# Sorting one batch item's values from both halves of the partitions, in a fused Sinkhorn attention and maxout kernel

## The chip, the cores and the metric

The kernel runs on one core of a Trainium2 chip. The metric is the device time of one execution in microseconds (us), lower is better; a result is the median of several executions, and beside it stands one execution taken with the hardware profiler. All input loads from HBM and the store of the output are within that time.

## What is computed

There are 4 batch items of 8 heads, 768 tokens and 64 dimensions a head. The tokens are cut into 8 blocks of 96. Five rounds of Sinkhorn turn each head's 8 x 8 `sort_net` into a mixing matrix P; keys and values are mixed block by block with P ("sorted"); each query block attends to the sorted block with its own number; the result, with the heads side by side, goes through a maxout layer.

```python
for _ in range(5):
    P = np.exp(P - np.max(P, axis=-1, keepdims=True))
    P = P / (np.sum(P, axis=-1, keepdims=True) + 1e-09)
    P = P / (np.sum(P, axis=-2, keepdims=True) + 1e-09)
k_sorted = np.einsum('bhij,bhjcd->bhicd', P, k_b)
v_sorted = np.einsum('bhij,bhjcd->bhicd', P, v_b)
attn = softmax(scale * q_b @ k_sorted^T)      # per block of 96
x = (attn @ v_sorted), heads side by side     # 3072 tokens x 512
out = np.maximum(x @ w1, x @ w2) @ w_out      # 512 -> 1024 -> 512
```

## The kernel before

**The algebra.** `max(h1, h2) = max(h1 - h2, 0) + h2`. So the kernel keeps W1 - W2 in place of W1 (`w_difference`), computes h = x (W1 - W2) with a ReLU as the eviction (`moe_h`, lines 591 to 617), and adds x (W2 Wout) to the output product. W2 Wout is made once: W2 is transposed on TensorE (`w2_transposes`, L553), then four products of 8 matmuls each (`w_product`, L571 to L584) fill PSUM two to a tile; each second product is followed by one eviction of 1024 columns into `wc`. An output tile of 128 tokens is 12 matmuls, 8 with g and 4 with x, in two parts of 6 (`moe_out`, L625).

**The sort on TensorE.** For a batch item the 64 rows (head, block) of v stand on 64 partitions: item b uses rows 0 to 63 if it is even and 64 to 127 if odd. `load_v` (L154) fills `v_raw`, and `turn_v` (L209) copies it to `v_dc` with d ahead of the token within the block. A sort is then, for each d, one matmul whose weights are 64 rows of `v_dc` (96 tokens, loaded 128 wide by `v_weights`) and whose moving operand is a 64 x 64 block diagonal matrix of P. `sort_v` (L411) does this for items 0 and 1, 16 values of d to a PSUM tile, all from one row half. `sort_v_pair` (L431) does it for items 2 and 3 together: 8 values of d from each row half, the halves in turn. `sort_k` (L387) sorts the keys from both halves in turn.

**The block diagonals.** `block_diagonals(b)` (L293) multiplies a selection matrix (`sel_v`, `sel_k`, made by `selections`, L281) with P on TensorE (L303), masks the result on VectorE with `maskJ` (L313), sums it (L320), and multiplies with `maskM` (L323) into bf16 matrices `bd`. For item 0 it runs ahead of everything; for items 1, 2 and 3 it runs in three calls. An even item's value matrix serves the next item too, since `sel_v` takes 16 columns of the identity: rows 0 to 63 get the even item's P and rows 64 to 127 the odd one's.

**Attention.** `scores` (L463) fills a PSUM tile for two heads and four blocks, ScalarE takes the exponential (L471), `values` (L490) multiplies with the sorted values and a column of ones, VectorE divides (L501, L507). `x_transposes` puts x under the features: on TensorE for item 0, by DMA transposes on the SP queue for the others. Queries come to `qT` by TensorE (items 0 and 1) or by DMA transposes (2 and 3).

**Engines and buffers.** Every PSUM tile (two banks) comes from one pool of four. Where no engine is given, `evac` asks `pick`, which keeps an estimate of the work waiting on ScalarE ("A") and VectorE ("D") and takes the lighter one. Loads with a conversion to bf16 are issued by GpSimd; output stores and transposes by SP. Each engine runs its instructions in the order of the program.

**The order of the work.** It is written out by hand for item 0 (lines 674 to 723). After that there is one list of units per item: 8 of `moe_h`, for item 0 four of `w_product`, then 12 half tiles of output. After each unit come the calls fixed in `tail` for its number, then as many `steps` of the next item's attention as are due. Due is what has the share of the steps that the units' costs so far have of the total cost:

```python
total = sum(cost[lo:-2])
want = -(-len(steps) * sum(cost[lo : n + 1]) // total)
```

In item 0's list (`lo` = 8) the 17 steps begin after unit 8, the first W2 Wout product: keys, two value sorts; after unit 9 the third value sort with half of the queries; after unit 10 the fourth with the other half, and the first scores. Items 1's and 2's lists start at units 2 and 4. A copy of item 1's half of the rows (`turn(second, ...)`, four calls) stands in `tail` after units 4 to 7; the copies of items 2 and 3 together (`turn(both, ...)`) go with the value steps of item 1.

Of the kernel before, what the change touches and what calls it, by code (L numbers as in the profile page):

```python
# [10 lines left out]
FP32 = mybir.dt.float32  # L11
BF16 = mybir.dt.bfloat16
# [4 lines left out]
def kernel(  # L17
# [16 lines left out]
    nc = tc.nc  # L34
# [7 lines left out]
    G = B * H  # L42
# [23 lines left out]
    def ps_f32(name):  # L66
        return psum.tile([128, 1024], FP32, tag="ps", name=name)
# [24 lines left out]
    def elapse(ns):  # L92
        for e in load:
            load[e] = max(0.0, load[e] - ns)
# [127 lines left out]
    def v_weights(rows, d):  # L222
        c = d // 2 * (2 * BLK) + d % 2
        return v_dc[rows, c : c + 255 : 2]
# [26 lines left out]


    id64 = const.tile([128, 64], FP32, tag="id64", name="id64")
    maskJ = const.tile([128, 2, NB], FP32, tag="maskJ", name="maskJ")
    maskM = const.tile([128, 2, 8], FP32, tag="maskM", name="maskM")

    def masks(part):
# [23 lines left out]
    def selections(b):  # L281
        src = ident[0:G, b * 8 : b * 8 + 8]
        if b % 2 == 0:
            sel_v[b] = const.tile([G, 16, NB], BF16, tag=f"sel_v{b}", name="sel_v")
            nc.vector.tensor_copy(
                out=sel_v[b], in_=ident[0:G, b * 8 : b * 8 + 16].to_broadcast([G, 16, NB])
            )
        sel_k[b] = const.tile([G, 8, 16], BF16, tag=f"sel_k{b}", name="sel_k")
        nc.vector.tensor_copy(out=sel_k[b], in_=src.to_broadcast([G, 8, 16]))

    bd_v, bd_k = {}, {}

    def block_diagonals(b):  # L293

        pe = ps_f32("pe")
        kinds = [1] if b % 2 else [1, 0]
        for m in kinds:
            sel = (
                sel_k[b].rearrange("g h w -> g (h w)")
                if m  # L300
                else sel_v[b].rearrange("g h j -> g (h j)")
            )
            nc.tensor.matmul(  # L303
                pe[:, m * 64 : m * 64 + 64],
                sel,
                p_bf.rearrange("p i j -> p (i j)"),
                start=True,
                stop=True,
            )
        n, m0 = len(kinds), min(kinds)  # L310
        both = slice(m0, m0 + n)
        pm = const.tile([128, n, NB, NB], FP32, tag=f"pm{n}", name="pm")
        nc.vector.tensor_tensor(  # L313
            out=pm,
            in0=pe[:, m0 * 64 : (m0 + n) * 64].rearrange("p (m i j) -> p m i j", i=NB, j=NB),
            in1=maskJ[:, both].to_broadcast([128, n, NB, NB]).transpose([0, 1, 3, 2]),
            op=ALU.mult,
        )
        pt = const.tile([128, n, NB], FP32, tag=f"pt{n}", name="pt")
        nc.vector.reduce_sum(out=pt, in_=pm, axis=AX.X)  # L320
        for m in kinds:
            bd = const.tile([128, 8, NB], BF16, tag=f"bd{m}{b}", name="bd")
            nc.vector.tensor_tensor(  # L323
                out=bd,
                in0=maskM[:, m].to_broadcast([128, 8, NB]),
                in1=pt[:, m - m0].to_broadcast([128, NB, 8]).transpose([0, 2, 1]),
                op=ALU.mult,
            )
            if m:
                bd_k[b] = bd.rearrange("p m i -> p (m i)")  # L330
            else:
                bd_v[b] = bd_v[b + 1] = bd.rearrange("p m i -> p (m i)")


    v_sb = big.tile([BLK, 128, D + 16], BF16, tag="v_sb", name="v_sb")
# [75 lines left out]
    def sort_v(b, t, n=0, eng=None):  # L411
        r0, m0 = (b % 2) * 64, (b % 2) * 64
        ps = ps_f32("v_ps")
        keep_streaming(ps, n)
        for m in range(16):
            d = t * 16 + m
            nc.tensor.matmul(  # L417
                ps[:, m * 64 : (m + 1) * 64],
                v_weights(slice(r0, r0 + 64), d),
                bd_v[b][r0 : r0 + 64, :],  # L420
                start=True,
                stop=True,
            )
        evac(
            v_sb[:, m0 : m0 + 64, t * 16 : (t + 1) * 16],
            ps[0:BLK].rearrange("p (d m) -> p m d", m=64),
            1024,
            eng=eng,
        )
# [136 lines left out]
            eng=eng,  # L566
        )

    wc_ps = {}

    def w_product(dmt):  # L571
        m = dmt % 2
        if m == 0:
            wc_ps[0] = ps_f32("wc_ps")
        for fb in range(NFB):
            nc.tensor.matmul(  # L576
                wc_ps[0][:, m * 512 : (m + 1) * 512],
                w2T[:, fb, dmt * 128 : (dmt + 1) * 128],
                wo_sb[:, fb, :],
                start=(fb == 0),  # L580
                stop=(fb == NFB - 1),
            )
        if m == 1:
            evac(wc[:, dmt - 1 : dmt + 1, :].rearrange("p t n -> p (t n)"), wc_ps[0], 1024)  # L584


    g_tiles = {}

# [94 lines left out]
            turn_v(first, "A", 18, 36)  # L683
    turn_v(first, "A", 36, 56)
    turn_v(first, "A", 56, 80)
    block_diagonals(0)
    turn_v(first, "D", 80, 96)

    SC, VA, TR = att(0)
# [31 lines left out]
    SC[7]()  # L721
    for b in range(1, B):
        selections(b)

    def turn(rows, c0):
        turn_v(rows, "D", c0, c0 + 24)
        load["D"] += 850

    def load_rest():
# [2 lines left out]

    tail = {
        2: [VA[6], TR[2], VA[7]],
        3: [TR[3], lambda: w2_transposes(1, "A")(), load_rest, lambda: block_diagonals(1)],
        4: [lambda: block_diagonals(2), lambda: turn(second, 0)],
        5: [lambda: block_diagonals(3), lambda: turn(second, 24)],
        6: [lambda: turn(second, 48)],
        7: [lambda: turn(second, 72)],
        9: [lambda: load_v(2), lambda: load_v(3), lambda: load_k(3)],  # L740
        14: [lambda: load_q(2)],
        18: [lambda: pair_q(2, 0), lambda: pair_q(2, 1), lambda: load_q(3)],
# [1 line left out]
    for b in range(B):  # L744
        units = [lambda t=t: moe_h(b, 0, t, None if b else "A") for t in range(4)]
        if b == 0:
            units[0] = lambda: None
            units[1] = lambda: None
        units += [lambda t=t: moe_h(b, 1, t) for t in range(4)]
        cost = [1.3] * 8  # L750
        if b == 0:
            units += [lambda dmt=dmt: w_product(dmt) for dmt in range(4)]
            cost += [1.7] * 4
        units += [
            lambda ti=ti, part=part: moe_out(b, ti, part)
            for ti in range(6 if b < B - 1 else 4)
            for part in range(2)
        ]
        cost += [1.3] * 12
        if b == B - 1:  # L760
            units += [
                lambda: moe_out_last(4, [(0, 512, "D")]),
                lambda: moe_out_last(5, [(0, 384, "D"), (384, 512, "A")]),
            ]
        steps, lo = [], 2
        if b < B - 1:
            qs = [lambda half=half: q_transposes(b + 1, half) for half in range(2)]
            ks = [lambda t=t, b=b: sort_k(b + 1, t) for t in range(3)]
            SC, VA, TR = att(b + 1)

            def group(*fs):
                return [lambda: [f() for f in fs]]

            if b == 0:
                lo = 8
                vs = [lambda t=t: sort_v(1, t) for t in range(4)]
                for m, c in enumerate((0, 24, 48, 72)):
                    VA[m + 1 : m + 2] = group(VA[m + 1], lambda c=c: turn(both, c))
                steps = group(*ks) + group(*vs[0:2]) + group(vs[2], qs[0]) + group(vs[3], qs[1])
            elif b == 1:  # L780
                vs = [lambda t=t: sort_v_pair(2, t) for t in range(8)]
                tail[0] = qs
                tail[10] = [lambda: pair_q(3, 0), lambda: pair_q(3, 1)]
                steps = group(*ks) + group(*vs[0:2]) + group(*vs[2:4]) + group(*vs[4:6])
                steps += group(*vs[6:8])
            else:
                tail[0] = qs
                lo = 4
                steps = group(*ks)
            steps += group(*SC[0:2]) + VA[0:1] + group(*SC[2:4]) + VA[1:2] + group(VA[2], TR[0])  # L790
            steps += group(*SC[4:6]) + VA[3:4] + group(VA[4], TR[1]) + group(*SC[6:8]) + VA[5:6]
            steps += group(VA[6], TR[2]) + VA[7:8] + TR[3:4]
        done = 0
        for n, unit in enumerate(units):
            elapse(1000 * cost[n] if n < len(cost) else 0)
            unit()
            for step in tail.get(n, []):
                elapse(250)
                step()
            total = sum(cost[lo:-2])  # L800
            want = -(-len(steps) * sum(cost[lo : n + 1]) // total)
            while done < min(want, len(steps)):
                elapse(250)
                steps[done]()
                done += 1
        tail = {}
# [28 lines left out]
```

## Time and profile before

| what | value |
|---|---|
| median of 3 executions | 172.62 us (172.55 to 173.13) |
| the profiled execution | 173.25 us |
| its span in the profile | 171.4 us |
| TensorE busy | 163.0 us |
| ScalarE busy | 84.6 us |
| VectorE busy | 78.5 us |
| GpSimd busy | 27.6 us |
| moved by DMA | 23.11 MB |

The span is the part of the profiled execution between the first and the last instruction of the profile. In the profile PE is TensorE's matmuls, PEld its weight loads (which overlap matmuls), DVE is VectorE, ACT is ScalarE, POOL is GpSimd, SP is SyncE, whose queue issues DMAs. L110 and L108 are `evac` on VectorE and ScalarE, whatever it copies: there the tile's name tells more. In a timeline row the columns are the start, the time from the first to the last of a run of equal instructions, the engine, the line, the operation, the tiles, the shapes and the count; a bracket tells how long the engine had been idle and what it waited for. "issue" is idle time in which the profile shows nothing that was waited for.

### The profile page before, as it was taken

How to read it: one execution, taken by the hardware profiler on the slowest of the kernel's cores; microseconds unless marked ns; L12 is line 12 of the kernel's file. 1: busy time of each engine (PE TensorE's matmuls, PEld its weight loads, DVE VectorE, ACT ScalarE, POOL GpSimd, SP SyncE). 2: the span in 40 equal slices, each digit the busy share in tenths (PEclk: the TensorE clock that was granted, in tenths of full speed). 3: DMA queues.
4: the chain of work that ended last, by engine and by line, in shares of the span. 5: the costliest groups of instructions: out<-in, count | busy, mean ns of one | idle time of the engine just before them, and what ended most of it. 6: DMA issues, size and time to landing. Idle time of an engine off the chain costs nothing.

```text
span 171.4 us, 4524 instructions
## 1 busy us (share of the span) xinstructions
PE 163.0 (95%) x1999; PEld 98.6 (58%) x2019; DVE 78.5 (46%) x177; ACT 84.6 (49%) x101; POOL 27.6 (16%) x44
## 2 busy tenths in 40 slices
PE   7999889999899999999999999999899999999992
PEld 7949655665756555557665455556555545554451
DVE  4978765949442688404854845005544410000011
ACT  3487568675656353247775332366634216552020
POOL 7865585222312002000000000000000000000000
PEclk9999999999999999999999999999999999999999
DMA  3999999999999986999300253693043663000333
GB/s 48 204 205 198 200 206 206 198 206 205 220 213 203 207 110 174 127 236 282 66 0 4 46 168 108 110 248 61 0 34 95 136 168 126 0 0 0 122 133 116
DMA packets 30244, 23.11 MB, mean 135 GB/s; under 512 B 16721, under 2 KB 25169, under 8 KB 30225
## 3 DMA queue, kind: packets, MB, share of 16 engines
q0 software_dynamic: 10880, 12.59, 44.0%
q1 hardware_dynamic: 19200, 10.17, 24.8%
q8 instruction: 16, 0.26, 0.6%
q10 hardware_dynamic: 144, 0.07, 0.1%
q14 instruction: 4, 0.02, 0.0%
HBM read 25.17 MB, written 6.29 MB: 184 GB/s over the span
## 4 chain that ended last, share of the span: by engine, by line
PE 83%; DVE 9%; ACT 3%; issue 2%; DMA 1%; DVEq 0%
PE out_ps L625 36%; PE h_ps L598 23%; PE wc_ps L576 4%; PE o_ps L490 4%; PE s_ps L463 4%; PE k_ps L396 3%; PE v_ps L417 2%; PE fill_ps L82 1%; PE v_ps L438 1%; DVE v_sb L110 1%; ACT e L471 1%; ACT kT L108 1%; PE tw_ps L553 1%; DVE qT L110 1%; DMA p_sb<-in_sort_net_dram 1%
## 5 line engine op out<-in xcount | busy, mean ns | idle before, releaser
L625 PE MATMUL out_ps<-wo_sb,g 128*128 128x512 bf16 (+2 forms) x188 | 46.1, 370 | 0.8 <-issue 0.3
L598 PE MATMUL h_ps<-xT,w_sb 128*128 128x384 bf16 x256 | 45.0, 326 | 0.8 <-DVE g L614 0.4
L471 ACT ACTIVATE e<-s_ps 96x768 bf16<-96x768 f32 x32 | 24.3, 803 | 20.8 <-PE s_ps L463 20.8
L598 PEld LDWEIGHTS <-w_sb 128*128 128x128 bf16 x256 | 23.9, 98 | 16.6 <-issue 1.1
L612 ACT ACTIVATE g<-h_ps 128x768 bf16<-128x768 f32 x27 | 21.9, 810 | 14.1 <-PE h_ps L598 14.1
L625 PEld LDWEIGHTS <-g 128*128 128x128 bf16 x200 | 17.3, 97 | 16.6
L108 ACT COPY o<-out_ps 128x1024 f32<-128x1024 f32 x10 | 10.1, 1012 | 29.9 <-PE out_ps L625 25.2
L625 PE MATMUL out_ps<-wc,xT 128*128 128x512 bf16 (+2 forms) x99 | 24.7, 370 | 0.1
L507 DVE TENSOR_TENSOR x<-o_ps,rs 96x512 bf16<-96x512 f32 x32 | 22.0, 687 | 1.1
L110 DVE CAST kT<-k_ps 128x1024 bf16<-128x1024 f32 x6 | 7.2, 1221 | 20.2 <-PE k_ps L396 20.2
L625 PEld LDWEIGHTS <-xT 128*128 128x128 bf16 x100 | 9.6, 97 | 11.2
L490 PEld LDWEIGHTS <-e 96*128 96x128 bf16 x256 | 11.3, 98 | 6.3 <-ACT e L471 1.2
L501 DVE RECIPROCAL rs<-o_ps 96x8 f32<-96x8 f32 x32 | 6.4, 200 | 17.9 <-PE o_ps L490 17.9
L660 DVE COPY o<-out_ps 128x512 f32<-128x512 f32 (+1 forms) x2 | 1.3, 626 | 28.9 <-PE out_ps L625 28.9
L110 DVE CAST v_sb<-v_ps 96x1024 bf16<-96x1024 f32 x9 | 11.0, 1217 | 5.2 <-PE v_ps L417 4.4
L490 PE MATMUL o_ps<-v_sb,e 96*128 96x65 bf16 x256 | 12.6, 193 | 0.4 <-ACT e L471 0.3
L463 PE MATMUL s_ps<-qT,kT 64*128 64x96 bf16 x256 | 9.3, 204 | 0.8 <-DVE qT L110 0.4
L463 PEld LDWEIGHTS <-kT 64*128 64x128 bf16 x256 | 6.4, 94 | 6.2 <-issue 5.7
L82 PEld LDWEIGHTS <-fill 128*128 128x128 bf16 x99 | 8.8, 123 | 1.8 <-DVE fill L73 1.2
L82 PE MATMUL fill_ps<-fill 128*128 128x138 bf16 x88 | 8.1, 277 | 1.2 <-DVE fill L73 1.2
L136 POOL DMA_DIRECT2D q_raw<-in_q_dram x7 | 5.5, 801 | 19.6 <-DVE q_pair L345 13.3
L149 POOL DMA_DIRECT2D k_raw<-in_k_dram x12 | 6.5, 543 | 8.3 <-DMA wo_sb<-in_moe_w_out_dram 4.7
(77 smaller groups left out, 139.7 us busy)
## 6 DMA issues: line engine op xcount, KB each, us to landing
out_dram<-o SPq DMA_DIRECT2D x11, 512.0 KB, 3.0
k_raw<-in_k_dram POOLq DMA_DIRECT2D x12, 256.0 KB, 12.3
v_raw<-in_v_dram POOLq DMA_DIRECT2D x6, 384.0 KB, 12.3
q_raw<-in_q_dram POOLq DMA_DIRECT2D x3, 768.0 KB, 9.9
w_sb<-in_moe_w_dram POOLq DMA_DIRECT2D x4, 256.0 KB, 9.8
w_sb<-in_moe_w_dram POOLq DMA_DIRECT2D x2, 512.0 KB, 11.1
wo_sb<-in_moe_w_out_dram POOLq DMA_DIRECT2D x2, 512.0 KB, 15.1
v_raw<-in_v_dram POOLq DMA_DIRECT2D x3, 256.0 KB, 5.1
```

Source lines behind the costliest of these rows:

```text
L82: nc.tensor.matmul(ps[:, 0:w], w0, fill[:, 0:w], start=True, stop=True)
L108: nc.scalar.copy(out=out_ap, in_=in_ap)
L110: nc.vector.tensor_copy(out=out_ap, in_=in_ap)
L149: nc.gpsimd.dma_start(out=k_raw[b][:, ci * n : (ci + 1) * n], in_=k_src[b, :, ci * n : (ci + 1) * n],)
L463: nc.tensor.matmul(ps[:, h2 * 512 + ii * 128 : h2 * 512 + ii * 128 + BLK], kT[b][rows, (hp * 8 + i) * BLK : (hp * 8 + i) * BLK + 128], rhs ...
L471: nc.scalar.activation(out=e[:, 0 : 8 * BLK].rearrange("p (t c r) -> p t c r", t=8, r=R), in_=ps[0:BLK] .rearrange("p (t f) -> p t f", t=8 ...
L490: nc.tensor.matmul(ps[:, h2 * 512 + ii * 65 : h2 * 512 + (ii + 1) * 65], e[:, (h2 * 4 + ii) * BLK : (h2 * 4 + ii) * BLK + 128], v_sb[:, m0 ...
L507: nc.vector.tensor_tensor(out=x, in0=ov[:, :, :, 0:D], in1=rs.to_broadcast([BLK, 2, 4, D]), op=ALU.mult,)
L576: nc.tensor.matmul(wc_ps[0][:, m * 512 : (m + 1) * 512], w2T[:, fb, dmt * 128 : (dmt + 1) * 128], wo_sb[:, fb, :], start=(fb == 0), stop=( ...
L598: nc.tensor.matmul(h_ps[t][:, m * 512 : m * 512 + TCH], w1_sb[:, hp, fb * 128 : (fb + 1) * 128], xT[:, b % 2, ch, hp % 2, hp // 2, :], sta ...
L612: nc.scalar.activation(out=g, in_=src, func=AF.Relu)
L625: nc.tensor.matmul(dst, g_tiles[b, ch, m // 2][:, m % 2, off : off + 128] if m < NFB else xT[:, b % 2, ch, hp % 2, hp // 2, off : off + 12 ...
```

## The change

It has these parts.

- Item 1's values are sorted by `sort_v_halved`, 8 values of d from each row half, the halves in turn. Rows 64 to 127 serve d = 0 to 31; d = 32 to 63 are copied by `halve_v`, one DMA on the SP queue, from rows 64 to 127 to rows 0 to 63 of `v_dc`. For that item 1 has a selection `sel_v[1]` with its own P in both halves, and a value matrix of its own.
- The four turns of item 1 stand after units 4 and 5, two each, and `halve_v` behind them.
- The block diagonals of items 1 to 3 are made in one call after unit 6, five in a row, with `maskJ` copied out to seven masks (two copies behind `selections`).
- `w_product` has a PSUM tile for each product and evicts it at once, 512 columns.
- Costs are whole numbers, the rule for the steps counts all units, item 1's list starts at unit 0, the sorts of the values of item 1 go two and two, the queries make a step of their own, and the last transposes go with the last values. Item 0's list then has 16 steps: keys and two value sorts after unit 8, the other two after unit 9, the queries after 10, the first scores after 11.

```diff
-    maskJ = const.tile([128, 2, NB], FP32, tag="maskJ", name="maskJ")
+    maskJ = const.tile([128, 7, NB], FP32, tag="maskJ", name="maskJ")
...
+        if b == 1:
+            sel_v[b] = const.tile([G, 16, NB], BF16, tag=f"sel_v{b}", name="sel_v")
+            for half in range(2):
+                nc.vector.tensor_copy(
+                    out=sel_v[b][:, half * 8 : half * 8 + 8], in_=src.to_broadcast([G, 8, NB])
+                )
...
-    def block_diagonals(b):
+    def block_diagonals(kinds, m0=0):
...
-        kinds = [1] if b % 2 else [1, 0]
-        for m in kinds:
+        n = len(kinds)
+        for c, (m, b) in enumerate(kinds):
...
-                bd_v[b] = bd_v[b + 1] = bd.rearrange("p m i -> p (m i)")
+                bd_v[b] = bd.rearrange("p m i -> p (m i)")
...
+    def halve_v():
+        half = slice(D // 2 * BLK, D * BLK)
+        nc.sync.dma_start(out=v_dc[0:64, half], in_=v_dc[64:128, half])
+
+    def sort_v_halved(b, t, eng=None):
+
+        ps = ps_f32("v_ps")
+        for m in range(8):
+            for par in range(2):
+                rows = slice(64 - par * 64, 128 - par * 64)
+                nc.tensor.matmul(
+                    ps[:, par * 512 + m * 64 : par * 512 + (m + 1) * 64],
+                    v_weights(rows, par * 32 + t * 8 + m),
+                    bd_v[b][rows, :],
+                    start=True,
+                    stop=True,
+                )
+        evac(
+            v_sb[:, 64:128, 0:D].rearrange("p m (par d) -> p par m d", par=2)[
+                :, :, :, t * 8 : (t + 1) * 8
+            ],
+            ps[0:BLK].rearrange("p (par d m) -> p par m d", par=2, m=64),
+            1024,
+            eng=eng,
+        )
...
     def w_product(dmt):
-        m = dmt % 2
-        if m == 0:
-            wc_ps[0] = ps_f32("wc_ps")
+        ps = ps_f32("wc_ps")
...
-        if m == 1:
-            evac(wc[:, dmt - 1 : dmt + 1, :].rearrange("p t n -> p (t n)"), wc_ps[0], 1024)
-
+        evac(wc[:, dmt, :], ps[:, 0:512], 512)
...
     for b in range(1, B):
         selections(b)
+    for c, n, m in [(2, 2, 0), (4, 3, 1)]:
+        nc.vector.tensor_copy(
+            out=maskJ[:, c : c + n],
+            in_=maskJ[:, m].to_broadcast([128, NB, n]).transpose([0, 2, 1]),
+        )
...
-        3: [TR[3], lambda: w2_transposes(1, "A")(), load_rest, lambda: block_diagonals(1)],
-        4: [lambda: block_diagonals(2), lambda: turn(second, 0)],
-        5: [lambda: block_diagonals(3), lambda: turn(second, 24)],
-        6: [lambda: turn(second, 48)],
-        7: [lambda: turn(second, 72)],
+        3: [TR[3], lambda: w2_transposes(1, "A")(), load_rest],
+        4: [lambda: turn(second, 0), lambda: turn(second, 24)],
+        5: [lambda: turn(second, 48), lambda: turn(second, 72), halve_v],
+        6: [lambda: block_diagonals([(0, 1), (0, 2), (1, 1), (1, 2), (1, 3)], 2)],
...
-        steps, lo = [], 2
+        steps, lo = [], 0
...
-                vs = [lambda t=t: sort_v(1, t) for t in range(4)]
+                vs = [lambda t=t: sort_v_halved(1, t) for t in range(4)]
...
-                steps = group(*ks) + group(*vs[0:2]) + group(vs[2], qs[0]) + group(vs[3], qs[1])
+                steps = group(*ks) + group(*vs[0:2]) + group(*vs[2:4]) + group(*qs)
...
-            steps += group(VA[6], TR[2]) + VA[7:8] + TR[3:4]
+            steps += group(VA[6], TR[2]) + group(VA[7], TR[3])
...
-            total = sum(cost[lo:-2])
+            total = sum(cost[lo:])
```

More of the change, by code (lines that the diff above doesn't have):

```diff
@@ L303, in block_diagonals @@
             nc.tensor.matmul(
-                pe[:, m * 64 : m * 64 + 64],
+                pe[:, c * 64 : c * 64 + 64],
                 sel,
@@ L309, in block_diagonals @@
             )
-        n, m0 = len(kinds), min(kinds)
-        both = slice(m0, m0 + n)
         pm = const.tile([128, n, NB, NB], FP32, tag=f"pm{n}", name="pm")
@@ L314, in block_diagonals @@
             out=pm,
-            in0=pe[:, m0 * 64 : (m0 + n) * 64].rearrange("p (m i j) -> p m i j", i=NB, j=NB),
-            in1=maskJ[:, both].to_broadcast([128, n, NB, NB]).transpose([0, 1, 3, 2]),
+            in0=pe[:, 0 : n * 64].rearrange("p (m i j) -> p m i j", i=NB, j=NB),
+            in1=maskJ[:, m0 : m0 + n].to_broadcast([128, n, NB, NB]).transpose([0, 1, 3, 2]),
             op=ALU.mult,
@@ L320, in block_diagonals @@
         nc.vector.reduce_sum(out=pt, in_=pm, axis=AX.X)
-        for m in kinds:
+        for c, (m, b) in reversed(list(enumerate(kinds))):
             bd = const.tile([128, 8, NB], BF16, tag=f"bd{m}{b}", name="bd")
@@ L325, in block_diagonals @@
                 in0=maskM[:, m].to_broadcast([128, 8, NB]),
-                in1=pt[:, m - m0].to_broadcast([128, NB, 8]).transpose([0, 2, 1]),
+                in1=pt[:, c].to_broadcast([128, NB, 8]).transpose([0, 2, 1]),
                 op=ALU.mult,
@@ L567, in w2_transposes @@
         )
-    wc_ps = {}
     def w_product(dmt):
-        m = dmt % 2
-        if m == 0:
-            wc_ps[0] = ps_f32("wc_ps")
+        ps = ps_f32("wc_ps")
         for fb in range(NFB):
             nc.tensor.matmul(
-                wc_ps[0][:, m * 512 : (m + 1) * 512],
+                ps[:, 0:512],
                 w2T[:, fb, dmt * 128 : (dmt + 1) * 128],
@@ L685 @@
     turn_v(first, "A", 56, 80)
-    block_diagonals(0)
+    block_diagonals([(0, 0), (1, 0)])
     turn_v(first, "D", 80, 96)
@@ L749 @@
         units += [lambda t=t: moe_h(b, 1, t) for t in range(4)]
-        cost = [1.3] * 8
+        cost = [13] * 8
         if b == 0:
             units += [lambda dmt=dmt: w_product(dmt) for dmt in range(4)]
-            cost += [1.7] * 4
+            cost += [17] * 4
         units += [
@@ L758 @@
         ]
-        cost += [1.3] * 12
+        cost += [13] * 12
         if b == B - 1:
@@ L791 @@
             steps += group(*SC[4:6]) + VA[3:4] + group(VA[4], TR[1]) + group(*SC[6:8]) + VA[5:6]
-            steps += group(VA[6], TR[2]) + VA[7:8] + TR[3:4]
+            steps += group(VA[6], TR[2]) + group(VA[7], TR[3])
         done = 0
         for n, unit in enumerate(units):
-            elapse(1000 * cost[n] if n < len(cost) else 0)
+            elapse(100 * cost[n] if n < len(cost) else 0)
             unit()
```

## The prediction

> **What bounds the kernel now.** I read the page's busy shares first, then the chain of work that ended last, then the timeline from 27 to 58 us, where the changed code runs, then the landing times of the SP queue's DMAs.
>
> ```profile
> PE 163.0 (95%) x1999; PEld 98.6 (58%) x2019; DVE 78.5 (46%) x177; ACT 84.6 (49%) x101; POOL 27.6 (16%) x44
> PE 83%; DVE 9%; ACT 3%; issue 2%; DMA 1%; DVEq 0%
> ```
>
> TensorE (PE) is the bound: busy 95% of 171.4 us, 83% of the chain; the other engines are at half. So each edit is worth what it takes from or adds to PE's row: its own instructions, the stops for a change of shape, and the waits that reach PE. The chain where the change works:
>
> ```profile
> 33.53 0.70 DVE x L507
> 34.27 0.51 PE tx_ps L528 x8
> ...
> 35.68 0.13 PE pe L303
> 35.81 1.41 PE h_ps L598 x8
> 37.22 0.16 PE pe L303 x2
> 37.38 1.41 PE h_ps L598 x8
> 38.78 0.13 PE pe L303
> 38.91 2.71 PE h_ps L598 x16
> ...
> 45.99 0.62 PE v_ps L417 x16
> ...
> 48.45 0.57 PE v_ps L417 x16
> ...
> 51.64 0.59 PE v_ps L417 x16
> ...
> 82.59 0.57 PE v_ps L438 x32
> ```
>
> Columns are start, length, what. The reader is to see: item 1's value sort (L417, one half of the rows) takes 0.57 to 0.62 us for 16 matmuls, while the pair sort of items 2 and 3 (L438, both halves in turn) takes 0.57 for 32; three small block diagonal products each stand between two units of h; and just before 34.27 the chain is on DVE. The waits of PE there, in brackets, and the DVE work that the new copy must follow, from the timeline:
>
> ```profile
> 37.26 0.96 DVE L614 TENSOR_SCALAR g<-h_ps 128x768 bf16<-128x768 f32 x1 [0.67 <-PE h_ps L598]
> ...
> 40.77 2.32 DVE L217 COPY v_dc<-v_raw 64x768 uint32<-64x768 uint32 x3
> ...
> 45.99 0.62 PE L417 MATMUL v_ps<-bd,v_dc 64*128 64x64 bf16 x16 [0.29 <-ACT kT L108]
> ...
> 53.52 0.35 PE L463 MATMUL s_ps<-qT,kT 64*128 64x96 bf16 x8 [0.25 <-DVE v_sb L110]
> ...
> 122.21 1.46 PE L598 MATMUL h_ps<-xT,w_sb 128*128 128x384 bf16 x8 [0.43 <-DVE g L614]
> ```
>
> **What the Trainium skill says.** "TensorE: Matmul & The Clock Gate", section "The mechanism": a weight load overlaps a matmul in flight only if it goes to another row group. The trace agrees: L438 spends 18 ns a matmul, L417 36 to 39. "TensorEngine Tiling (Array Packing)", "Key Properties": a change of tiling mode drains TensorE. The trace agrees: 24 matmuls of h in a row take 3.90 us, 1.30 a unit of 8, and a unit after a stop for another shape 1.41, so 0.11 a stop. "DMA: Bandwidth & Descriptors", "Issuing engines are not separate DMA queues": DMAs of SP, ACT and GpSimd share the same 16 engines and interleave. The trace agrees: 512 KB to HBM from SP landed in 2.8 to 3.5 us with few loads about, in 3.9 and 6.7 us (issued at 75.94 and 70.27) beside a load from GpSimd.
>
> **The change, part by part.** The profiled execution took 173.25 us (span 171.4 and 1.85 around it), 0.63 over the median of 172.62; I make the sum against it and carry the difference to the median.
>
> 1. **Value sort of item 1.** Before: 0.62 (at 45.08), 0.62, 0.57, 0.59, in all 2.40 us for 64 matmuls. After, the same number and shape alternate between the row halves as L438 does. Its first group, straight after the keys, took 0.79 (80.40 to 81.19) for 32, the others 0.57: 1.36. **-1.04**, all on PE. The results leave PSUM in the pair sort's shape at its 1.22 (DVE) or 1.00 us (ACT), as now: nothing.
> 2. **Tiles of W2 Wout, and the order of steps.** There are four PSUM tiles. One W2 Wout tile is held through two units, from 41.6 to 48.4, with key tiles in the other three. Hence a wait of 0.09 before 45.08 and one of 0.29 at 45.99. With a tile each, evacuated at once, the fifth tile is free after about 0.6 us (512 columns; 1024 take 1.01 on ACT), before the keys end 1.64 us later. The 0.25 at 53.52 is a score waiting for the tile of the last value sort (DVE until 53.48); after the change the values are two units earlier. **-0.63**; -0.2 if other tiles take their place. Four evacuations of 0.6 for two of 1.0 and 1.2 lie on engines half idle.
> 3. **Block diagonals.** Before: three stops, 0.13 + 0.16 + 0.13, and 0.11 each for the next unit: 0.75. After: one of five matmuls, 0.13 + 4 x 0.03, and 0.11: 0.36. **-0.39**. On DVE they now come behind all four turns: a product and a sum of 320 elements (128 take 0.29, 64 take 0.22: about 0.47 each) and five writes at 0.18. The third is item 1's key matrix, ready near 43.1; the keys want it at 43.2. The value matrix, last, is ready near 43.5, wanted at 44.9. Nothing, but the cover is thin: 0.3 if I am that far off.
> 4. **Selections and masks.** Four more small DVE copies run after 31.9, before the last two value steps of item 0. That stretch is on the chain: DVE's selections, reciprocals and x end at 34.22, and PE's transpose starts at 34.27, its weight load having waited 0.46. A selection of 128 elements costs 0.13; the two new of 64 and the two mask copies of 16 and 24 I put at 0.07 to 0.08 each (bounds 0.25 and 0.5 in all): **+0.30**.
> 5. **More stops.** Queries apart from the last values in item 0's loop, and keys apart from values in item 1's: two stops at 0.11, **+0.22**. Value steps cost no stop (the output unit after one takes 1.30).
> 6. **Item 2's loop.** I worked the planner's rule by hand for every unit. The value step and the two scores, both after unit 6 now, split to units 6 and 7, so the tile that unit 7 waits for (0.43 at 122.21) is an earlier one. **-0.30**, a little left for a value step's DVE work.
> 7. **The copy of half of d.** It is 64 rows of 6144 bytes, 384 KB inside SBUF, on the SP queue, which has nothing before it and nothing behind it until the first transpose (60.33 in the trace before). It waits for the last turn. That turn's DVE work starts behind item 0's g (end 38.22, moved by +0.30 - 0.24 to 38.28): 3 x 0.77 + 0.83 = 3.15, so 41.45, issue at 41.5. The first value sort takes both halves at once and stands on PE behind the keys, at 44.99 + 0.30 - 0.39 = 44.9. The copy is hidden if it lands within 3.4 us; every bit beyond stalls PE, with everything queued behind it. No row before shows a plain copy within SBUF (the x transposes, 96 KB each, land in 2.8 to 7.0 but in small packets). An 8 KB load landed in 1.8; with 512 KB at 2.8, 3.9 and 6.7, three quarters of the bytes gives 2.6, 3.4 and 5.5. The DMA engines are full from 42 to 46 us (busy share 1.16), so not 2.6; between the loaded ones the middle is 4.4, and I take 4.0, as the target is not HBM. **+0.6**; bounds 0 (a gain is excluded: nothing waits for this copy today) and, unscaled, 3.3.
>
> Sum: -1.04 - 0.63 - 0.39 + 0.30 + 0.22 - 0.30 = -1.84 without the copy, -1.24 with it. 173.25 becomes 172.0; from the median, 171.4.
>
> Moved without price, and their cover: the turns of item 1 run one behind the other, and no other PSUM result needs DVE meanwhile (units 5 to 7 go to ACT). GpSimd's load of item 3's values waits for those turns, over 1 us earlier than now. The last x transposes come a unit or more later: item 2's after unit 18, with 1.3 + 4 x 1.3 = 6.5 us until they are read, against 1.2 for DVE and SP and 2.8 to 4.3 to land. Tightest is item 1's second, after unit 18 and two q copies on DVE: about 6.2 us for a landing that took 3.5 when quiet and 7.0 at 70.69. If late, +0.75.
>
> **Rivals.**
> - *Lands in time.* The copy stays under 3.4 us: -1.84, **170.8**. For: unloaded, 512 KB took 2.8. Against: the full DMA engines.
> - *Break-even.* It lands in 4.7 to 5.8 us and gives nearly everything back: **172.6**. For: the scaled 5.5.
> - *Slower.* Same place, the wait of the first value sort for the copy behind the loads of items 2 and 3: from 5.2 us on the whole is a loss, from 5.8 one of 0.3%. At the 6.7 of 70.27: -1.84 + 3.3, **174.1**. For: that landing. Against: it had two transposes in its own queue.
> - *Given back later.* The copy behaves, but the tile waits only move (+0.43) and the late transpose costs 0.75: **172.6**. For: tight numbers in 2 and 7. Against: PE was idle 0.25 of the 25 us from 75 to 100, where values are sorted with the same tiles.
> - That the halves don't overlap is excluded by L438.
>
> **How the numbers follow.** Copy 3.4 to 4.7 (171.4; own range 170.8 to 172.1): 0.40. In time: 0.22. Break-even: 0.16. Slower: 0.14. Given back: 0.08, half of it over the bound. About 0.3%, 0.5 us, is what a measurement can tell from no change. Faster 0.62, same 0.20, slower 0.18. The range 170.5 to 173.4 leaves out the far end of the late copy and a best case in which also parts 4 and 5 cost nothing.
>
> **What will show it.** The 16 matmuls of a halved sort in about 0.3 us; five block diagonal products in one place; PE's wait ahead of the first halved sort, put down to the copy, 0.6 us, and the copy's landing, 4 us; the transpose of 34.27 at about 34.6; no waits of PE at the old 45.99, 53.52 and 122.21. I am wrong if the copy takes over 5 us, if turns end later than 41.5, or if a wait on x transposes shows up in h.

## The result, and the profile after

The changed kernel is slower: 178.09 us (177.28 to 179.47, four runs) against 172.88 (172.55 to 173.19); ratio 1.031, 95% interval 1.023 to 1.039. The forecast was 171.4, range 170.5 to 173.4. Here and below the ratio leaves out any execution more than 1.5% above the fastest of its kernel, while medians and ranges keep it; that is one execution each of 'unread', 'dve_shift' and 'best'.

The profiled execution took 179.47 us, the slowest of the four, and 6.22 more than that of before. From the page of the changed kernel: TensorE's busy time and share, the clock granted to it in 40 slices of 4.4 us, and the queue that fetches instructions.

```profile
PE 162.5 (91%) x2002; PEld 96.3 (54%) x2020; DVE 76.3 (43%) x177; ACT 86.0 (48%) x104; POOL 30.2 (17%) x44
PEclk9999999999957999999999999999999999999999
q8 instruction: 16, 0.26, 0.6%
```

PE is busy as long as before (162.5 us, before 163.0) in a longer span, and two slices, from 48.8 to 57.7 us, have a lower clock. A DMA has come into the chain there (start, length, what), from the changed kernel:

```profile
38.47 3.08 DVE v_dc L217 x4
...
41.64 9.02 DMA v_dc<-v_dc
...
52.49 2.77 PE wc_ps L602 x6
55.26 0.58 PE v_ps L445 x32
55.84 1.83 PE wc_ps L602 x8
```

The turns end at 41.55 and the copy is issued by 41.64, both within 0.15 us of the forecast. It lands after 9.02 us. PE came to the first halved sort at 44.99 (forecast 44.9) and stood for 5.51 us. Behind the wait everything is slow for a while: the first 31 matmuls of the sort take 1.03 us where the second 32 take 0.58, and six matmuls of W2 Wout take 2.77 where eight take 1.83.

By the start of each item's first h product, the difference to the kernel before is +6.15 for item 1 (81.01 against 74.86), +6.74 for item 2 (116.29 against 109.55) and +6.27 for item 3 (148.30 against 142.03). So item 1's list loses 0.59, item 2's gives 0.47 back, and all else happens before item 1's first h product, nearly all of it behind item 1's keys (43.35 against 43.28). From the timeline of the changed kernel, PE's new waits:

```profile
34.73 0.51 PE L558 MATMUL tx_ps<-ident,x 96*128 96x96 bf16 x8 [0.45 <-DVE x L537]
...
50.70 1.03 PE L445 MATMUL v_ps<-bd,v_dc 64*128 64x64 bf16 x31 [5.51 <-DMA v_dc<-v_dc]
...
74.92 1.47 PE L649 MATMUL out_ps<-wo_sb,g 128*128 128x512 bf16 x5 [0.26 <-DVE x L537]
...
90.36 0.24 PE L468 MATMUL v_ps<-bd,v_dc 64*128 64x64 bf16 x4 [0.52 <-issue]
```

The first is the forecast cost of the four DVE copies, the second the wait for the copy. In the third an output unit that takes a new PSUM tile waits for VectorE's x; the kernel before has no such wait. The fourth was not forecast either: a stop in the midst of 32 like matmuls, 28 before it and 4 behind it, for which the profile shows no reason.

### The profile page after: what moved, and what is told of

It reads as the page before. It is cut to its first block, busy times and chain, and to the rows that moved or that the text cites. A ratio compares the mean times of both kernels' runs of the same rounds, so it can differ in the third digit from the quotient of the medians.

```text
span 177.6 us, 4536 instructions
## 1 busy us (share of the span) xinstructions
PE 162.5 (91%) x2002; PEld 96.3 (54%) x2020; DVE 76.3 (43%) x177; ACT 86.0 (48%) x104; POOL 30.2 (17%) x44
## 4 chain that ended last, share of the span: by engine, by line
PE 75%; DVE 12%; DMA 6%; ACT 2%; issue 2%; SPq 0%
PE out_ps L649 34%; PE h_ps L622 20%; DMA v_dc<-v_dc 5%; PE wc_ps L602 4%; PE o_ps L520 4%; PE s_ps L493 4%; PE k_ps L400 3%; DVE v_dc L217 2%; PE v_ps L468 1%; DMA p_sb<-in_sort_net_dram 1%; ACT e L501 1%; PE tq_ps L375 1%; DVE x L537 1%; PE tw_ps L583 1%; DVE qT L110 1%
## 5 line engine op out<-in xcount | busy, mean ns | idle before, releaser
L649 PE MATMUL out_ps<-wo_sb,g 128*128 128x512 bf16 (+2 forms) x188 | 47.0, 370 | 1.1 <-issue 0.3
L108 ACT COPY o<-out_ps 128x1024 f32<-128x1024 f32 x11 | 11.1, 1012 | 40.4 <-issue 22.8
L110 DVE CAST v_sb<-v_ps 96x1024 bf16<-96x1024 f32 x8 | 9.7, 1218 | 10.8 <-PE v_ps L445 8.6
L520 PE MATMUL o_ps<-v_sb,e 96*128 96x65 bf16 x256 | 13.1, 193 | 0.4 <-ACT e L501 0.3
L108 ACT CAST v_sb<-v_ps 96x1024 bf16<-96x1024 f32 x8 | 8.0, 1005 | 7.2 <-PE v_ps L445 5.2
L110 DVE CAST kT<-k_ps 128x1024 bf16<-128x1024 f32 x5 | 6.0, 1222 | 12.1 <-PE k_ps L400 12.1
L136 POOL DMA_DIRECT2D q_raw<-in_q_dram x7 | 6.4, 935 | 24.6 <-DVE rs L531 14.0
L602 PE MATMUL wc_ps<-wo_sb,w2T 128*128 128x512 bf16 x29 | 9.0, 441 | 0.3 <-issue 0.2
L82 PEld LDWEIGHTS <-fill 128*128 128x128 bf16 x99 | 7.5, 111 | 1.8 <-DVE fill L73 1.2
## 6 DMA issues: line engine op xcount, KB each, us to landing
v_raw<-in_v_dram POOLq DMA_DIRECT2D x6, 384.0 KB, 14.6
```

Source lines behind the costliest of these rows:

```text
L82: nc.tensor.matmul(ps[:, 0:w], w0, fill[:, 0:w], start=True, stop=True)
L108: nc.scalar.copy(out=out_ap, in_=in_ap)
L110: nc.vector.tensor_copy(out=out_ap, in_=in_ap)
L136: nc.gpsimd.dma_start(out=t[:, hs], in_=src[:, hs])
L520: nc.tensor.matmul(ps[:, h2 * 512 + ii * 65 : h2 * 512 + (ii + 1) * 65], e[:, (h2 * 4 + ii) * BLK : (h2 * 4 + ii) * BLK + 128], v_sb[:, m0 ...
L602: nc.tensor.matmul(ps[:, 0:512], w2T[:, fb, dmt * 128 : (dmt + 1) * 128], wo_sb[:, fb, :], start=(fb == 0), stop=(fb == NFB - 1),)
```

## Experiments

Theory 1: the copy lands late among the loads, PE stands still, and the standing still itself halves the clock; the rest of the change gains about what was forecast. Rivals: the clock drop has another cause (called 2 in the first run); the new order of steps is a loss (called 2 in the second and third runs); the copy's traffic delays the loads (3); a copy across the halves is slow by itself (4). The stops without a reason brought in theory 5, instruction fetch, against 6, PSUM or data.

### PE kept busy while it waits

```diff
         ps = ps_f32("v_ps")
+        keep_streaming(ps, 12288 if t == 0 else 0)
         for m in range(8):
```

> The changed kernel, with 24 matmuls of zeros (128x512, about 0.22 us each, 5.2 us in all) put on TensorE ahead of the first halved value sort, so that TensorE is busy while the copy is under way. Theory 1 (the copy lands 9 us after its issue, TensorE stands still 5.5 us, and the standing still also halves its clock for the next 6 us, worth about 2.2 us): 178.1 - 2.2 = 175.9 us, clock at full speed throughout. Theory 2 (the half clock has another cause than the idle time, or only the wait counts): 178.1 us, half clock still there. In both the copy lands some 9 us after its issue.

Measured: **175.92 us** (175.55 to 176.54; the kernel before, run beside it, 172.79; ratio 1.018, 1.016 to 1.021). From this kernel's timeline:

```profile
44.91 5.35 PE L82 MATMUL v_ps<-fill 128*128 128x512 bf16 x23
...
50.60 0.64 PE L446 MATMUL v_ps<-bd,v_dc 64*128 64x64 bf16 x31 [0.20 <-DMA v_dc<-v_dc]
```

The zeros fill the wait, the copy again lands after 9.0 us, the clock stays full, and 2.17 us are gone by the medians. Theory 1's second half holds: the half clock follows from standing still, as the Trainium skill says ("TensorE: Matmul & The Clock Gate", section "What's actually happening": about 3.4 us of idling throttle the array to half). The trace agrees: in the changed kernel PE idles from 45.2, and its clock is half from 48.4, 3.2 us later, to 55.2. The price is read best in the traces: from item 1's keys to item 1's first h product the changed kernel takes 37.50 us and 'fill' 35.38, so the clock is worth 2.1 us. In item 1's list 'fill' saves another 0.70, where the stop of 90.36 is gone as well.

### The copy issued, but not read

```diff
-                vs = [lambda t=t: sort_v_halved(1, t) for t in range(4)]
+                vs = [lambda t=t: sort_v(1, t) for t in range(4)]
```

> The changed kernel with the copy issued as before, but item 1's values sorted from rows 64 to 127 alone as in the kernel before, so nothing waits for the copy. Theory 1 (the wait for the copy is the whole loss; the other parts gain): parts 2 to 6 of the prediction, -0.80, and about 0.5 lost in item 1's list, so 172.3 us, with the copy still landing after some 9 us. Theory 2 (the new order of steps is itself a loss): 174 us or more. Theory 3 (the copy's traffic delays the loads, and these the work): over 173.5 us, with waits of TensorE on loads.

Measured: **175.67 us** (174.23 to 176.90; ratio 1.014, 1.009 to 1.018). By its time this would be theory 2 or 3, but the trace shows the cause of neither. The wait for the copy is gone. The four executions spread over 2.7 us, and the profiled one, the quickest, has a stop in the second pair of value sorts, behind its sixth matmul. (Its mean clock is 0.998; the other three have 0.980 to 0.990, so they may have stood longer, but of them there is no trace.) From its timeline:

```profile
47.36 0.35 PE L421 MATMUL v_ps<-bd,v_dc 64*128 64x64 bf16 x6
...
49.66 0.93 PE L421 MATMUL v_ps<-bd,v_dc 64*128 64x64 bf16 x26 [1.95 <-issue]
```

No load shows among PE's waits, so theory 3 doesn't explain the time. The copy does delay loads: those of the values (384 KB) land after 15.2 us in the median here and 14.6 in the changed kernel, against 12.3 before and 12.7 in the next run, which has no copy.

### No copy: VectorE writes both halves

```diff
...
+            for rows, d0, d1 in [(slice(64, 128), 0, 17), (slice(0, 64), 16, 32)]:
+                dst = v_dc[rows, 0 : D * BLK].bitcast(U32).rearrange("p (d c) -> p d c", c=BLK)
+                nc.vector.tensor_copy(out=dst[:, d0:d1, c0:c1], in_=src[:, d0:d1, c0:c1])
...
```

(called for four groups of columns from rows 64 to 127 of `v_raw`, in place of the turns and of `halve_v`; 17 pairs of d are written, since the weights are loaded wider than the 96 tokens; the 16 of rows 0 to 63 are read from rows 64 to 127).

> The changed kernel without the copy: VectorE's four turns of item 1 write one half of d to rows 64 to 127 and the other half straight to rows 0 to 63, as two instructions a turn of about half the size. Theory 1: all of the predicted gain, -1.84, less about 0.5 in item 1's list, so 171.5 us, no wait ahead of the first halved sort. Theory 2 (the new order of steps is a loss): 174 us or more.

Measured: **173.46 us** (173.24 to 173.68; ratio 1.0042, 1.0029 to 1.0055). From its timeline:

```profile
44.08 1.71 PE L400 MATMUL k_ps<-bd,k_raw 64*64 64x64 bf16 x96 [0.94 <-DVE bd L327]
...
49.95 0.56 PE L449 MATMUL v_ps<-bd,v_dc 64*128 64x64 bf16 x26 [1.27 <-issue]
```

The time lies between the two theories, and two waits stand where the gain should be. The keys wait 0.94 for the block diagonals: the eight smaller turns take 4.17 us, not 3.1, and the block diagonals are behind them (the "thin cover" of part 3). And there is the same stop behind the sixth matmul of the second pair (26 of the 32 follow it).

### The values later

```diff
-                steps = group(*ks) + group(*vs[0:2]) + group(*vs[2:4]) + group(*qs)
+                steps = group(*ks) + group(*qs) + group(*SC[0:2])
+                steps += group(*vs[0:2]) + group(*vs[2:4])
...
-            steps += group(*SC[0:2]) + VA[0:1] + group(*SC[2:4]) + VA[1:2] + group(VA[2], TR[0])
+            if b:
+                steps += group(*SC[0:2])
+            steps += VA[0:1] + group(*SC[2:4]) + VA[1:2] + group(VA[2], TR[0])
```

> The changed kernel with its copy, but in item 0's list the queries and the first scores come ahead of the value sorts (keys, queries, scores, values, values), which puts some 5.7 us of other TensorE work between the keys and the first value sort. Theory 1 (only the wait counts): the wait for the copy falls below 0.5 us, the clock stays full, 171.7 us. Theory 3 (the copy's traffic delays the loads): the queries' load, which lands near 44 us, or others hold TensorE up, 174 us or more.

Measured: **176.51 us** (175.94 to 177.29; ratio 1.023, 1.019 to 1.027). The copy is hidden, as theory 1 says (it lands at 48.8, the values follow at 55.0), but a stop of 3.47 us, and half the clock behind it, take its place. It isn't the queries' load, which landed at 43.9. From its timeline:

```profile
44.19 1.47 PE L375 MATMUL tq_ps<-ident,q_raw 128*64 128x128 bf16 x46
...
49.13 0.25 PE L375 MATMUL tq_ps<-ident,q_raw 128*64 128x128 bf16 x2 [3.47 <-issue]
```

This place gave theory 5. Here 46 query transposes stand between the keys and the stop; in the two kernels above it is 32 value matmuls, 8 of W2 Wout and 6 of values: 46 too. The stop goes with the number of the instruction, not with its data. The 16 packets of queue q8 carry 0.26 MB, 16 KB each, and the page of the changed kernel counts 2002 matmuls and 2020 weight loads on PE, 251 to a packet. The Trainium skill ("Runtime: NRT & Kernel Launch", "Instruction fetch mechanics") has instructions fetched by DMA in blocks of 16 KiB, 256 instructions, and calls the cost of a block "mostly hidden". If theory 5 holds it is not hidden here: the three stops are 1.27, 1.95 and 3.47 us. 256 instructions are 128 pairs of weight load and matmul; a "cut" below is the place in the program where one block ends and the next begins.

### The blocks of instructions cut elsewhere

```diff
-    keep_streaming(ps_f32("fill_ps"), 88 * 138, most=138)
+    keep_streaming(ps_f32("fill_ps"), 24 * 506, most=506)
```

> The kernel 'unread', with TensorE's warming matmuls at the start as 24 of 506 columns in place of 88 of 138: the same time on TensorE, but 64 matmuls (128 instructions) fewer ahead of all that follows. In 'unread' TensorE stopped 1.9 us after the 46th matmul behind the keys, in 'dve' 1.3 and in 'late' 3.5 us after the same one, though the matmuls there are of other kinds. Theory 5 (TensorE has run out of fetched instructions; its instructions come by DMA in pieces of 16 KB, 256 of them, and wait among the loads): the stop leaves this place and 173 us or less is measured. Theory 6 (the stop is a wait for a PSUM tile or for data): the stop stays, 175.7 us.

> The kernel 'dve' with the same 64 matmuls fewer at the start. Theory 5 (instruction fetch): the stop of 1.3 us in the second pair of value sorts goes, 173.5 - 1.3 = 172.2 us. Theory 6: the stop stays, 173.5 us.

Measured: **175.91 us** (174.40 to 176.00) and **175.44 us** (173.84 to 177.43), beside 172.72 before (ratios 1.017 and 1.013). The forecast times were missed, and the place was hit: no stop is left behind item 1's keys. New ones stand in item 0's value sort. From the timeline of 'unread_shift', then of 'dve_shift':

```profile
18.91 0.52 PE L421 MATMUL v_ps<-bd,v_dc 64*128 64x64 bf16 x12 [1.27 <-issue]
...
83.00 0.59 PE L468 MATMUL v_ps<-bd,v_dc 64*128 64x64 bf16 x28 [1.62 <-issue]
```

```profile
19.72 0.52 PE L421 MATMUL v_ps<-bd,v_dc 64*128 64x64 bf16 x12 [1.94 <-issue]
```

Counted in the program from item 0's first key matmul, the old stop is behind 628 matmuls. With 64 fewer ahead of it, cuts 128 apart fall at 692, 564, 436, 308 and 180; the new stop is behind 181. The stop in item 1's list moved as well, from behind the 28th matmul of the third group of 32 (the changed kernel) to behind the 4th of the second: 28 values, 8 of h and 28 values back, 64, which on a grid of 128 is the same as 64 on. These counts agree with a grid of 128 to within two matmuls. Theory 5 fits all of it, and theory 6 none of it.

### Both together, with selections and block diagonals early

```diff
-    w2_transposes(0, "D")()
-    w_difference(3)
-    SC[7]()
     for b in range(1, B):
         selections(b)
...
+    w2_transposes(0, "D")()
+    w_difference(3)
+    SC[7]()
...
+            lambda: block_diagonals([(0, 1), (0, 2), (1, 1), (1, 2), (1, 3)], 2),
...
-        6: [lambda: block_diagonals([(0, 1), (0, 2), (1, 1), (1, 2), (1, 3)], 2)],
```

(This comes on top of 'dve'. The selections and mask copies now stand ahead of the first W2 transposes, and the block diagonals at the end of the calls after unit 3. 'best' has the 24 warming matmuls, 'best0' the 88.)

> The kernel 'dve_shift', with the selections and mask copies ahead of the first W2 transpose's eviction, where VectorE was idle 1.0 us, and the five block diagonals behind the second W2 transpose, ahead of the turns. If the waits that stand in 'dve' for block diagonals (0.9 us) and for x before the last TensorE transposes (0.4 us) are real costs: 172.2 - 0.9 - 0.4 = 170.9 us, faster than the kernel before. If they only cover other waits: 172 us or more.

> The kernel 'best' with the 88 warming matmuls of before, so that the pieces of TensorE's instructions are cut as in 'dve': VectorE writes both row halves, selections early, block diagonals ahead of the turns. Theory 5 (instruction fetch): no stop in item 0's value sort, but the one of 'dve' again after the 46th matmul behind item 1's keys, somewhat longer, since TensorE comes there about 1 us sooner and the fetch does not: 173.5 - 0.4 = about 173 us (172.3 to 173.5). Theory 6 (the stops are chance or PSUM): 172.1 us, no stop.

Measured: **173.66 us** for 'best' (172.05 to 174.90, twenty runs; ratio 1.0036, 1.0013 to 1.0059), which stops 1.64 us in item 0's value sort; and **170.62 us** for 'best0' (170.18 to 170.84; 172.60 before; ratio 0.9888, 0.9870 to 0.9905). 'best0' is faster than both kernels. That its gain of 1.98 us is near the forecast 1.84 is luck: it has steps moved that the change leaves in place, and 'single' below gets most of it without the paired sort. My expectation for 'best0' was wrong: no stop of the kind is in its trace.

The traces show what differs. The stop's place is a cut; one cut, that is 128 matmuls, ahead of it lies 14 matmuls into item 1's keys, and one packet of queue q8 follows there. In 'dve', 'unread' and 'late' it comes 3.2 to 3.6 us after that earlier cut (in 'dve' at 47.55, the cut at 44.32), and PE goes on 2.4 to 3.0 us after the packet. In 'best0', 'best2', 'single' and the kernel before it comes 0.9 to 1.2 us after the cut (in 'best0' at 43.35, the cut at 42.47), and none of these four kernels stops at that place. (In the changed kernel and in 'fill' it is 3.2 us late too, but there PE reaches the stop's place only after the wait for the copy.) So a cut in a dense stretch makes a stop possible, and a late packet goes with a stop; what makes the packet late is not shown.

### One more unit between keys and values

```diff
-                steps = group(*ks) + group(*vs[0:2]) + group(*vs[2:4]) + group(*qs)
+                steps = group(*ks) + group() + group(*vs[0:2]) + group(*vs[2:4]) + group(*qs)
```

> The kernel 'best0' with an empty step behind item 1's keys, so that the two pairs of value sorts come one unit later each, one W2 Wout product between the keys and the first and one between the two, the queries and the first scores together: the 256 instructions of the piece in question then last about 1.2 us longer on TensorE. Theory 5: the stop shrinks by about that, or goes; 171 to 171.8 us. Theory 6: as 'best0', within 0.3 us.

Measured: **170.52 us** (170.25 to 170.71; ratio 0.9877, 0.9862 to 0.9891), not to be told from 'best0'. With no stop to remove, the run decides nothing.

### The copy by itself

The kernel before gets a copy into a tile that nothing reads, behind item 1's last turn and again in item 3's list.

```diff
+        n = D // 2 * BLK // part
+        a = v_dc[rows_in, D // 2 * BLK : D // 2 * BLK + n]
+        b = scr[rows_out, 0:n]
+        nc.sync.dma_start(
...
-        7: [lambda: turn(second, 72)],
+        7: [lambda: turn(second, 72), lambda: probe(second, first)],
...
-        tail = {}
+        tail = {2: [lambda: probe(second, first)]} if b == 2 else {}
```

> The kernel before, with two added copies of the change's size and shape (64 rows of 6144 bytes from partitions 64 to 127 to partitions 0 to 63) into a tile that nothing reads: one on the SP queue behind item 1's last turn, near 43 us and beside the loads, one in item 3's list near 146 us with no load about. Theory 1 (the copy waits its turn among the loads' packets on the same DMA engines): 8 to 9.5 us to landing beside the loads, 2.5 to 3.5 us without. Theory 4 (a copy within SBUF from one half of the partitions to the other is slow by itself): 8 us or more both times. The time stays at 172.8 us within 0.5.

> The kernel before with two added copies that nothing reads: beside the loads, near 43 us, 64 rows of 3072 bytes, half of the change's copy in as many pieces; in item 3's list, in a stretch without any other DMA, the whole 64 rows of 6144 bytes. If each row's piece waits its turn among the loads' packets, half the bytes take nearly as long as all, 8 us or more; if the bytes count, about 5.5 us. In the quiet stretch: under 4.4 us, since the first probe had a store of 512 KB 0.15 us behind it; about 3 us.

Time from issue to landing, from the traces: the whole copy beside the loads (issued at 42.6) and in item 3's list (143.0), first probe:

```profile
DMA to landing us min/median/max: 9.7/9.7/9.7
...
DMA to landing us min/median/max: 4.4/4.4/4.4
```

Half the bytes in as many rows beside the loads (43.1), second probe; its quiet copy again took 4.4:

```profile
DMA to landing us min/median/max: 8.7/8.7/8.7
```

Theory 4 falls: without loads the same copy takes less than half. It takes 4.4 and not the 2.5 to 3.5 expected, but both quiet copies had an output store about 0.4 us ahead of them, so 4.4 is an upper bound of what it takes alone. Half the bytes save 1.0 us of 9.7, so the bytes are not what the time beside the loads goes by. That each of the 64 rows waits its turn among the loads' packets fits, but no run changed the number of rows, so that is not shown. The two executions took 173.09 and 173.66 us; nothing waits for the copies.

### The pairing alone

'best0' with item 1's values sorted from one half, and nothing copied:

```diff
-        4: [lambda: turn_halves(0), lambda: turn_halves(24)],
-        5: [lambda: turn_halves(48), lambda: turn_halves(72)],
+        4: [lambda: turn(second, 0), lambda: turn(second, 24)],
+        5: [lambda: turn(second, 48), lambda: turn(second, 72)],
...
-                vs = [lambda t=t: sort_v_halved(1, t) for t in range(4)]
+                vs = [lambda t=t: sort_v(1, t) for t in range(4)]
```

> The kernel 'best0' without its paired sort: item 1's values are turned and sorted in rows 64 to 127 alone, 16 values of d to a tile, as in the kernel before, and nothing is copied; the order of steps, the W2 Wout tiles, the early selections and early block diagonals stay. If the pairing is worth what the prediction's part 1 says (1.04 us): 170.6 + 1.0 = 171.6 us. If the gain of 'best0' is that of the order and tiles alone: 170.6 us, within 0.3.

Measured: **171.00 us** (170.61 to 171.24; 172.72 before; ratio 0.9892, 0.9872 to 0.9912). It lies between the two expectations. The medians differ by 0.38 us; each against its own before, 'best0' gains 1.98 and 'single' 1.72; and the two ratios are almost equal. So 0.1 to 0.4 us of the whole time is all that shows of the pairing, and these runs can't tell it from nothing. Theory 2, that the new order of steps is a loss, falls here: with this order and without the pairing the kernel is 1.7 us faster than before. The timelines of 'single' and then of 'best0':

```profile
43.59 1.10 PE L421 MATMUL v_ps<-bd,v_dc 64*128 64x64 bf16 x32
```

```profile
43.87 0.64 PE L449 MATMUL v_ps<-bd,v_dc 64*128 64x64 bf16 x32
44.75 1.89 PE L606 MATMUL wc_ps<-wo_sb,w2T 128*128 128x512 bf16 x7 [0.24 <-DVE kT L110]
```

The paired sort takes 0.46 us less for 32 matmuls, 0.9 in all. But PE then comes sooner to the next tile and waits 0.24 for a key tile's eviction, which the slower sort covers. From item 1's keys to item 1's first h product 'best0' takes 29.98 us, 'single' 30.61 and the kernel before 31.42: in the traces the pairing is worth 0.63 there, and the order and the tiles 0.81.

## Why the prediction was wrong, point by point

**Part 7 failed, and it is the step that decided.** It put the landing at 4.0 us by scaling stores of 512 KB by their bytes, and its bound at 6.7. It measured 9.0, and 9.7 as a probe. The bytes were the wrong measure: half of them land after 8.7. The largest landing in the trace before should not have been the end of the range for a kind of DMA that it does not show. That trace also had a warning nearer by: the two loads of 384 KB issued at 41.9 and 43.4, in the very stretch of the copy, took 11.9 and 12.3 us to land. The rival "slower" had the right place and sign, and it decides from where the prediction put it, but its price was 3.3 us; the wait alone is 5.5.

**A cost that no part had: the clock.** The prediction priced a wait as its own length. A PE that stands for 5.5 us here pays 2.1 us more ('fill').

**Part 1** was right in its rate (0.57 us for 32; the first group didn't take the 0.79 that was put). In 'best0' the sorts take 1.15 us for 2.40 before, even more than the 1.04 forecast. But 0.32 of it needs no second half: 'single' sorts 32 in a row from one half in 1.04 us, 2.08 in all. The pairing itself saves 0.93, of which a tile wait of 0.24 takes a part, and of the whole time no more than 0.4 shows.

**Part 2**: the waits of 0.29 at 45.99, 0.25 at 53.52 and the small one before 45.08 are not in the trace of 'best0'; one of 0.24 for a key tile is, and one of 0.26 at 66.29 for VectorE's x (74.92 in the changed kernel). So by the waits 0.13 of 0.63, near the -0.2 that it gave for other tiles taking their place.

**Parts 3 and 4** came in as put: five products in one place; the transpose at 34.73 with a wait of 0.45, for 34.6 (from the h unit ahead of it to the transpose it is 0.36 longer than before, for 0.30). The thin cover of part 3 held in the changed kernel (keys at 43.35, as before) and gave way, for 0.94, as soon as the turns took 1 us longer ('dve').

**Part 5** was right: a unit behind a stop takes 1.41.

**Part 6** was right: item 2's list takes 0.47 less, for 0.30.

**The sum.** From item 1's keys to item 1's first h product the changed kernel takes 37.50 us, 6.08 more than before (31.42). Less 5.5 for the wait and 2.1 for the clock that is a gain of 1.5, where parts 1 and 2 and one stop of part 5 were to give 1.56. Item 1's list then loses 0.59 (0.52 of it the stop) and item 2's gains 0.47. So the gains came in nearly as forecast in sum, if not part by part, and the copy, with the clock, is what turned them into a loss. Runs without the copy say the same: with 0.94 and 1.27 of waits taken off that 'dve' had of its own, 173.46 becomes 171.25, a gain of 1.5 against 172.79 by subtraction. 'best0' measures 1.98 under its own before, but with its early selections it also saves 0.60 ahead of the x transposes against the changed kernel (part 4).

**"Given back later"** had one place right, a tile wait that only moved (0.26 at 74.92), and one wrong: no wait for an x transpose shows in h. More is given back by the supply of instructions (0.52 at 90.36), which no part of the prediction had looked at.

Open: why the fetch's packet comes about 1 us after the cut in some kernels and over 3 us in others, and how much of the spread of the changed kernel (2.2 us) is the copy's landing and how much the fetch.

## What to carry to other kernels

A DMA put between two steps of a busy engine is to be priced as that kind of DMA, beside the loads that run at that time, and not by its bytes alone; if no trace shows it, a probe that nothing reads costs one run. If the copy only moves data across partitions, the engine that writes it first may put it in both places. When a stretch of small matmuls is made shorter, look whether its instructions come fast enough: a stop marked "issue" that kept its place in the count of instructions, whatever the instructions were, was fetch here, and shifting the count showed it. And a change made of several parts needs a run without the part that names it: here most of the gain was there without the pairing.

## What the runs showed of the hardware that I had not expected

- TensorE's instructions come in 16 KB pieces over the same DMA engines as the loads (16 packets of queue q8); with these full, dense stretches of weight loads and matmuls ran out of instructions for 0.3 to 3.5 us, at cuts 128 matmuls apart.
- A copy of 384 KB within SBUF took 8.0 to 9.7 us beside full loads (six traces), half of it 8.7, and 4.4 beside one store.
- VectorE can write rows 0 to 63 from rows 64 to 127 at the pace of a copy that stays in its rows: 384 elements of 32 bits a row in 0.49 us, beside 408 in 0.53 ('dve'). A turn of 768 in one instruction takes 0.83.
